# Power tables in channel-pair order, x loaded by segment, and the lag bounce split by PSUM bank, in a kernel of gated attention and a long convolution

## The chip, the cores and the metric

The kernel runs on one core of one Trainium2 chip. Its time is the device time of one execution in microseconds (us). Before the change the median of three runs was 586.04 us (585.66 to 587.24). One further execution was profiled; it took 592.4 us, and the trace of it spans 590.6 us.

## The reference

The result is `g * a + (1 - g) * b` over x with 2048 tokens and 512 channels, where g is a sigmoid of x times gate_w, one number for each token. Cut to what matters:

```
a: 32 heads of 16, four segments of 512 tokens
   in each segment: causal softmax attention, plus a linear-attention read of a
   memory M that holds phi(k)^T v of the segments before; mixed by sigmoid(beta)
   the result times wo
b: K[d, l] = Re sum_n C[d,n] * exp(dt[d] * A[d,n] * l_rounded_to_bf16) * dt[d] * B[d,n]
   y = causal convolution over the 2048 tokens of u[:, d] with K[d, :], by FFT
   b = y + u * Dskip          (u is x)
```

The lag index l goes through bfloat16, so lags beyond 256 are rounded and the kernel needs only five blocks of 128 of them.

## The kernel before, in words

There are three bodies of work.

**Attention.** `do_xT` transposes a segment of x on TensorE. `project`, `seg_tokens`, `seg_state`, `group`, `ophase` and `oproj` do the rest by segment and by eight heads; the exponentials of `group` (L1030) are 160 instructions of 128x1024 on ScalarE. `project` leaves its keys in SBUF through L985 (ScalarE) and L986 (VectorE). `oproj` writes its product, scaled by the token gate, through two SBUF buffers to a DRAM tensor, scr_abuf (L1113 and the DMA behind it). `gate_tokens` computes the token gate for all four segments at once, writes it to DRAM (scr_gbuf), reads it back in another order, and L914 on VectorE takes 1 minus it.

**Tables and lags.** z = exp(dt*A) and its powers z^(2^k), k = 0 to 10, come from `ssm_powers`: per power a tile of three planes (re, im, -im), each 512 columns, one column per channel, with the 128 states n on the partitions. `tables(c)` is called for each of four blocks of 128 channels. It builds a table F of 32 entries and a table G of 49 entries; an entry is a power of z, re and im, for 128 channels. Each of 15 calls of `cmul` makes up to 8 entries out of earlier ones, with three VectorE instructions: product with re (L1145), crossed product with im into a tile t2 (L1148), and the sum (L1151). Then come the lag products: for each channel two matmuls (re and im) with the channel's 32 entries of F as weights and its 49 entries of G as moving data give the 32x49 lags of K for that channel. Those are 256 matmuls for each block, in four PSUM banks of 8 slots by 4 column groups, each bank copied out by L1191. A table holds entry after entry, 128 channels each, so the 32 or 49 values that one matmul reads lie 128 elements (256 bytes) apart in a partition. The lags go to DRAM (scr_K) with one DMA of 392 KB for each block and come back with one DMA in channel order (kd). L1196 and L1199 rearrange kd into a tile kl, five transposes (L1206) and L1209 put it in KTT. Tile kl is taken from the pool of t2.

**x levels and tail.** `x_level1` is the first level of the transform of x, written to DRAM (scr_Z). `tail` loads scr_Z and constants into memory that the tables held before; for t = 0 to 15 it multiplies transform constants with KTT (L1246, L1247), transforms Z (L1263), multiplies both (L1267, L1269, L1271), transforms back, evacuates to a tile V (L1282 or L1284), and stores V to DRAM (scr_V). Every fourth t it loads V2 from there. Last comes the final level with the gate (L1306, L1320).

**What sets the order.** Every instruction is an `op` with an engine, an estimated cost, a key and the tiles it touches. A list scheduler in `Sched.schedule` simulates the engines with those costs and writes each engine's instructions down in the order in which it started them; of those ready at once the lowest key goes first. On the chip each engine works through its own list in order, with semaphore waits. All DMAs are issued by the SP queue, in order too. A tile pool hands its buffers out strictly in the order in which the program asked for tiles: `if self.queue[self.qpos] is not tile or not self.free: return None`. Pools that share memory have phases; a later phase's pool waits until the earlier one's is done. A part of the lines around the change:

```
t2P = mkpool("t2", 4096, 3)
kl = Tile(t2P, BF16)
a = T0            # the prep tiles (pb, ft, xk ...) lie over F, G and t2
KEYS = (12, 6, 50, 70)
```

Of the kernel before, what the change touches and what calls it, by code (L numbers as in the profile page):

```python
# [8 lines left out]
BF16 = mybir.dt.bfloat16  # L9
# [5 lines left out]
NDMA = 110  # L15
KEYS = (12, 6, 50, 70)
# [502 lines left out]
def f_exp(f):  # L519
    if f < 16:  # L520
        return 4 * f
    if f < 24:
        return 2 + 4 * (f - 16)
    return 1 + 2 * (f - 24)
# [51 lines left out]
def build_kernel(nc, A_x, A_wq, A_wk, A_wv, A_wo, A_beta, B_A_re, B_A_im, B_B_re, B_B_im,  # L576
                 B_C_re, B_C_im, B_log_dt, B_Dskip, gate_w, out):
    with contextlib.ExitStack() as es:
# [39 lines left out]
        gzT = S.keep(64, F32)  # L618
        gcolT = S.keep(64, F32)
        g4T = S.keep(64, F32)  # L620
# [7 lines left out]
        smP = S.pool("small", S.addr, 128, 8)  # L628
        S.addr += 8 * 128
# [8 lines left out]
        xTP = mkpool("xT", 4096, 4)  # L638
# [12 lines left out]
        pTP = mkpool("pT", 2048, 8)  # L651
# [3 lines left out]
        oTP = mkpool("oT", 1024, 6)  # L655
# [4 lines left out]
        t2P = mkpool("t2", 4096, 3)  # L660
        T1 = a
        pwP = mkpool("pw", 3072, 11)
# [3 lines left out]
        assert a <= 207 * 1024, a  # L666

        a = T0
# [3 lines left out]
        xkP = mkpool("xk", 4096, 4, 0)  # L672
# [5 lines left out]
        a = T1 + 33792 + 2048  # L678
# [7 lines left out]
        K3P = mkpool("K3", 3072, 2, 2)  # L686
# [3 lines left out]
        VP = mkpool("V", 2048, 2, 2)  # L690
# [37 lines left out]
        xk = []  # L728
        for s in range(4):
            T = Tile(xkP, BF16)  # L730
            S.dma(lambda T=T: ap(T, dims=[[512, 4], [1, 512]]),
                  lambda s=s: bass.AP(x.tensor, x.offset + s * 4 * 128 * 512, [[512, 128], [128 * 512, 4], [1, 512]]),
                  524288, w=[T], key=(-0.95 if s == 0 else 1.0 + s))
            xk.append(T)
# [13 lines left out]
        def do_xT(s):  # L748
            S.tag = "xT"
            T = Tile(xTP, BF16)  # L750
            parts = []
            for hb in range(2):
                P = S.ps(dt=BF16)

                def f(e, P=P, hb=hb):
                    for t2 in range(2):
                        for k in range(4):
                            i = e.transpose(ap(P, t2 * 512 + k * 128, n=128), ap(xk[s], (2 * hb + t2) * 512 + k * 128, n=128), ap(ident, n=128))
                    return i
                op("PE", 8 * 0.07, f, r=[xk[s], ident], w=[P])  # L760
# [51 lines left out]
        def plane(T, i, c0=0, n=512):  # L812
            return ap(T, i * 512 + c0, n=n)

        def ssm_powers(pb, dt, zr, zi):
            S.tag = "pow"
            A = lambda T: ap(T, n=512)
            for k in range(11):
                pw = Tile(pwP, BF16)
                op("ACT", c_act(512), lambda e, pw=pw, zr=zr: e.activation(plane(pw, 0), A(zr), ACT.Copy), r=[zr], pw=[pw])  # L820
                op("ACT", c_act(512), lambda e, pw=pw, zi=zi: e.activation(plane(pw, 1), A(zi), ACT.Copy), r=[zi], pw=[pw])
                op("ACT", c_act(512), lambda e, pw=pw, zi=zi: e.activation(plane(pw, 2), A(zi), ACT.Copy, scale=-1.0), r=[zi], pw=[pw])
# [12 lines left out]
        def ssm_cb(pb, dt):  # L835
# [7 lines left out]
            op("DVE", 0.69, lambda e: e.tensor_tensor(ap(CBT, n=512), A(u1), A(u2), ALU.subtract), r=[u1, u2], pw=[CBT])  # L843
            op("DVE", 0.69, lambda e: e.scalar_tensor_tensor(A(u1), A(pb[4]), -1.0, A(bi), ALU.mult, ALU.mult), r=[bi, pb[4]], w=[u1])
            op("DVE", 0.69, lambda e: e.tensor_tensor(A(u2), A(pb[5]), A(br), ALU.mult), r=[br, pb[5]], w=[u2])
            op("DVE", 0.69, lambda e: e.tensor_tensor(ap(CBT, 512, n=512), A(u1), A(u2), ALU.subtract), r=[u1, u2], pw=[CBT])
            P = S.ps()
            op("PE", c_mm(512), lambda e: mm(e, ap(P, n=512), ap(onesT, n=128), ap(CBT, n=512), True, True), r=[onesT, CBT], w=[P])
# [6 lines left out]
        dK = DT()  # L855
# [39 lines left out]
        def gate_tokens():  # L895
# [3 lines left out]
            def mkf(s):  # L899
                def f(e):  # L900
                    for tb in range(4):
                        for k in range(4):
                            i = mm(e, ap(P, 4 * s + tb, n=1), ap(xT[s], k * 512 + tb * 128, n=128), ap(gwT, k, n=1), k == 0, k == 3)
                    return i
                return f
            for s in range(4):
                op("PE", 0.9, mkf(s), r=[xT[s], gwT], pw=[P])
# [508 lines left out]
```

## Time and profile before

| what | value |
|---|---|
| time, median of 3 runs | 586.04 us |
| profiled execution: time, span | 592.4 us, 590.6 us |
| TensorE busy | 451.5 us (76%), 3837 matmuls |
| VectorE busy | 377.3 us (64%) |
| ScalarE busy | 371.7 us (63%) |
| mean granted TensorE clock | 0.777 |
| DMA | 46.03 MB, 64297 packets |

A row of the timeline gives start and length in us, engine, line, operation and shape; a bracket at its end says how long the engine had been idle before, and who released it. A timeline row with x4 is four instructions from the first one's start to the last one's end. A row of the groups gives busy time in us and the mean in ns, then idle time before them. All matmuls but two kinds run through one helper, L715, so they are told apart by shape: 128x49 on 128*32 weights is the lag product. A row of the windows gives the stretch, its length, then busy time of each engine with the number of instructions that fall into it, and the granted clock.

### The profile page before, as it was taken

How to read it: one execution, taken by the hardware profiler on the slowest of the kernel's cores; microseconds unless marked ns; L12 is line 12 of the kernel's file. 1: busy time of each engine (PE TensorE's matmuls, PEld its weight loads, DVE VectorE, ACT ScalarE, POOL GpSimd, SP SyncE). 2: the span in 40 equal slices, each digit the busy share in tenths (PEclk: the TensorE clock that was granted, in tenths of full speed). 3: DMA queues.
4: the chain of work that ended last, by engine and by line, in shares of the span. 5: the costliest groups of instructions: out<-in, count | busy, mean ns of one | idle time of the engine just before them, and what ended most of it. 6: DMA issues, size and time to landing. Idle time of an engine off the chain costs nothing.

```text
span 590.6 us, 9127 instructions
## 1 busy us (share of the span) xinstructions
PE 451.5 (76%) x3837; PEld 225.3 (38%) x3837; DVE 377.3 (64%) x569; ACT 371.7 (63%) x405; POOL 5.0 (1%) x17
## 2 busy tenths in 40 slices
PE   5846639999888889986998964989945897877080
PEld 3323213336643238534358421358412443323020
DVE  3757738995629998679993379927401395645063
ACT  5989838989864867682899531898744564545000
POOL 1000000000000000000000000000000000000000
PEclk9866677999595765796995585885986899889576
DMA  8600013330190000700000700020999977544616
GB/s 243 166 1 2 2 36 108 116 109 27 16 77 1 0 1 1 29 28 17 21 1 2 34 22 0 2 68 1 101 122 169 359 210 194 158 139 158 158 50 167
DMA packets 64297, 46.03 MB, mean 78 GB/s; under 512 B 28160, under 2 KB 59392, under 8 KB 64000
## 3 DMA queue, kind: packets, MB, share of 16 engines
q1 hardware_dynamic: 64256, 45.44, 36.5%
q8 instruction: 30, 0.49, 0.4%
q14 instruction: 11, 0.09, 0.1%
HBM read 31.23 MB, written 14.20 MB: 77 GB/s over the span
## 4 chain that ended last, share of the span: by engine, by line
PE 28%; DVE 22%; ACT 18%; DMA 18%; SPq 9%; issue 4%; DVEq 0%; ACTq 0%
PE psum L715 27%; SPq L248 9%; ACT sb L1030 6%; DMA scr_V<-sb 5%; ACT sb L1191 5%; DVE sb L1151 5%; DMA scr_K<-sb 4%; DVE sb L1148 4%; DVE sb L1145 4%; DMA sb<-scr_K 2%; DMA scr_gbuf<-sb 2%; DMA sb<-scr_V 2%; DVE sb L1282 1%; DVE sb L879 1%; DMA sb<-in_A_wq_dram 1%
## 5 line engine op out<-in xcount | busy, mean ns | idle before, releaser
L715 PE MATMUL psum<-sb 128*32 128x49 bf16 (+12 forms) x3601 | 432.2, 384 | 115.7 <-ACT sb L1030 24.2
L715 PEld LDWEIGHTS psum<-sb 128*128 128x128 bf16 (+5 forms) x3601 | 207.2, 155 | 335.1 <-issue 123.7
L1030 ACT ACTIVATE sb<-psum 128x1024 bf16<-128x1024 f32 x160 | 189.3, 1236 | 42.5 <-PE psum L715 41.4
L1148 DVE TENSOR_TENSOR sb<-sb 128x2048 bf16<-128x2048 bf16 (+3 forms) x60 | 50.7, 844 | 3.1 <-PE psum L1206 3.1
L1151 DVE TENSOR_TENSOR sb<-sb 128x2048 bf16<-128x2048 bf16 (+3 forms) x60 | 51.0, 850 | 1.8
L1145 DVE TENSOR_TENSOR sb<-sb 128x2048 bf16<-128x2048 bf16 (+3 forms) x60 | 50.4, 845 | 0.1
L1191 ACT ACTIVATE sb<-psum 128x392 bf16<-128x392 f32 x16 | 32.6, 2108 | 3.5 <-PE psum L715 3.5
L1097 DVE CAST sb<-psum 128x512 bf16<-128x512 f32 x16 | 28.6, 1790 | 9.6 <-PE psum L715 9.6
L1113 ACT ACTIVATE sb<-psum,sb 128x512 bf16<-128x512 f32 x16 | 10.9, 687 | 35.6 <-DMA scr_abuf<-sb 20.8
L1246 ACT ACTIVATE sb<-psum 128x1024 bf16<-128x1024 f32 x16 | 16.4, 1023 | 22.5 <-PE psum L715 22.5
L1320 DVE SCALAR_TENSOR_TENSOR sb<-psum,sb 128x512 bf16<-128x512 f32 x16 | 10.9, 744 | 23.5 <-DMA sb<-scr_abuf 18.5
L1081 DVE TENSOR_SCALAR sb<-psum 128x32 f32<-128x32 f32 x12 | 2.2, 187 | 35.8 <-PE psum L715 35.8
L1044 ACT ACTIVATE sb<-psum 128x512 bf16<-128x512 f32 x32 | 19.1, 596 | 5.8 <-PE psum L715 5.7
L1263 ACT ACTIVATE sb<-psum 128x1024 bf16<-128x1024 f32 x16 | 16.2, 1020 | 7.1 <-PE psum L715 3.7
L1282 DVE CAST sb<-psum 128x1024 bf16<-128x1024 f32 x8 | 9.8, 1221 | 15.8 <-DMA scr_V<-sb 12.2
L986 DVE TENSOR_SCALAR sb<-psum,sb 128x512 bf16<-128x512 f32 x16 | 11.8, 745 | 9.0 <-ACT sb L985 8.9
L1062 DVE RECIPROCAL sb<-psum 128x32 f32<-128x32 bf16 x16 | 5.7, 355 | 17.0 <-PE psum L1057 16.9
L982 ACT ACTIVATE sb<-psum 128x512 bf16<-128x512 f32 x16 | 9.5, 596 | 11.0 <-PE psum L715 11.0
L1284 ACT ACTIVATE sb<-psum 128x1024 bf16<-128x1024 f32 x8 | 8.2, 1024 | 11.0 <-PE psum L715 5.6
L985 ACT ACTIVATE sb<-psum,sb 128x512 bf16<-128x512 f32 x16 | 10.9, 684 | 6.5 <-PE psum L715 6.4
L877 ACT ACTIVATE sb<-psum 128x1024 bf16<-128x1024 f32 x8 | 8.2, 1025 | 10.2 <-PE psum L715 10.2
L934 DVE CAST sb<-psum 128x512 bf16<-128x512 f32 x16 | 14.0, 884 | 0.9 <-PE psum L715 0.9
(83 smaller groups left out, 286.1 us busy)
## 6 DMA issues: line engine op xcount, KB each, us to landing
sb<-c_D SPq DMA_DIRECT2D x16, 320.0 KB, 4.4
sb<-in_A_x_dram SPq DMA_DIRECT2D x32, 128.0 KB, 4.1
scr_Z<-sb SPq DMA_DIRECT2D x16, 256.0 KB, 2.2
sb<-scr_Z SPq DMA_DIRECT2D x32, 128.0 KB, 7.3
scr_V<-sb SPq DMA_DIRECT2D x16, 256.0 KB, 3.1
sb<-scr_V SPq DMA_DIRECT2D x16, 256.0 KB
sb<-in_A_x_dram SPq DMA_DIRECT2D x4, 512.0 KB, 7.7
scr_abuf<-sb SPq DMA_DIRECT2D x16, 128.0 KB, 2.5
```

The lines of the kernel that those rows point to most:

```text
L248: return self.op("SP", 0.06, lambda e: e.dma_start(out(), in_(), **kw), r=r, w=w, pw=pw, key=key, lat=lat)
L715: mm = lambda e, o_, l, r_, st, sp, **kw: e.matmul(o_, lhsT=l, rhs=r_, start=st, stop=sp, skip_group_check=True, **kw)
L1030: op("ACT", c_act(1024), lambda e, P=P, pT=pT: e.activation(ap(pT, n=1024), ap(P, n=1024), ACT.Exp, scale=0.25), r=[P], w=[pT])
L1044: op("ACT", c_act(512), lambda e: e.activation(ap(raw, n=512), ap(PV, n=512), ACT.Copy), r=[PV], w=[raw])
L1097: op("DVE", c_dps(512), lambda e: e.tensor_copy(ap(oT, n=512), ap(P3, n=512)), r=[P3], w=[oT])
L1145: op("DVE", c_tt(256 * n), lambda e: e.tensor_tensor(D_(), ap(tile, src * 128, [[pl, 2], [128 * sstep, n], [1, 128]]), ap(pw, d0, [[0, 2], ...
L1148: op("DVE", c_tt(256 * n), lambda e: e.tensor_tensor(T_(), ap(tile, pl + src * 128, [[-pl, 2], [128 * sstep, n], [1, 128]]), ap(pw, sg[0] ...
L1151: op("DVE", c_tt(256 * n), lambda e: e.tensor_tensor(D_(), D_(), T_(), ALU.add), r=[t2], w=wr)
L1191: op("ACT", c_act(392), lambda e, P=P, bk=bk: e.activation(ap(kex, bk * 392, n=392), ap(P, n=392), ACT.Copy), r=[P], pw=[kex])
L1246: op("ACT", c_act(1024), lambda e, PK=PK, K3=K3: e.activation(ap(K3, dims=[[1024, 2], [1, 512]]), ap(PK, dims=[[512, 2], [1, 512]]), ACT.C ...
L1263: op("ACT", c_act(1024), lambda e, PX=PX, Xs=Xs: e.activation(ap(Xs, dims=[[256, 2], [512, 2], [1, 256]]), ap(PX, dims=[[512, 2], [256, 2] ...
L1282: op("DVE", c_dps(1024), lambda e, PI=PI, V=V: e.tensor_copy(ap(V, n=1024), ap(PI, n=1024)), r=[PI], w=[V])
```

## The change

1. **Tables by channel pair.** F and G are stored as [re/im][64 channel pairs][entry][2 channels]. The power tiles become [block][re, re, im, -im][128 channels], 4096 bytes where they had 3072; the two copies of re are one ScalarE instruction and -im comes from VectorE. The lag matmuls then read 32 and 49 values that lie 2 elements (4 bytes) apart. `cmul` keeps its three VectorE instructions and their sizes, with innermost runs of 2 elements in the first two and of 2n in the sum. G holds im first; the sign of the crossed product is the same for F and G. The two interleaved quarters of F become two blocks, and `f_exp` is changed to suit.
2. **x by segment.** x is loaded to one buffer (four before) a segment at a time; `do_xT` and `gate_tokens` are called for each segment inside the attention loop; xT has 2 buffers (4 before). The DMAs of the token gate and L914 come with the last segment.
3. **Lag bounce by bank.** Each block's scr_K store becomes four, one behind each bank's copy; the DRAM dependence is kept by block. Tile kl is taken from the pool of kex, not of t2.
4. **Buffers.** t2 2 (from 3), pT 7 (8), oT 5 (6), small 6 (8); in the tail K3 3 (2) and V 4 (2). The prep tiles lie over G and t2 only, no longer over F.
5. **Planner.** The assumed cost of a lag matmul is 0.04 us (0.033).

```diff
@@ cmul
-                D_ = lambda: ap(tile, dst * 128, [[pl, 2], [128 * dstep, n], [1, 128]])
-                T_ = lambda: ap(t2, dims=[[n * 128, 2], [128, n], [1, 128]])
-                sg = (1, 512) if conj else (2, -512)
-                op("DVE", c_tt(256 * n), lambda e: e.tensor_tensor(
-                    D_(), ap(tile, src * 128, [[pl, 2], [128 * sstep, n], [1, 128]]),
-                    ap(pw, d0, [[0, 2], [0, n], [1, 128]]), ALU.mult), r=rd + [pw], w=wr + [tile])
...
+                run = lambda T, E, e0, st: ap(T, 2 * e0, [[2 * E, 128], [2 * st, n], [1, 2]])
+                pwv = lambda i: ap(pw, c * 512 + i * 256, [[2, 128], [0, n], [1, 2]])
+                op("DVE", c_tt(256 * n), lambda e: e.tensor_tensor(run(tile, ne, dst, 1), run(tile, ne, src, sstep), pwv(0), ALU.mult),
+                   r=rd + [pw], w=wr + [tile])
+                op("DVE", c_tt(256 * n), lambda e: e.tensor_tensor(run(t2, n, 0, 1), run(tile, ne, src, sstep), pwv(1), ALU.mult),
+                   r=rd + [pw], w=[t2])
+                D_ = lambda: ap(tile, 2 * dst, [[ne * 128, 2], [2 * ne, 64], [1, 2 * n]])
                 op("DVE", c_tt(256 * n), lambda e: e.tensor_tensor(
-                    D_(), D_(), T_(), ALU.add), r=[t2], w=wr)
+                    D_(), D_(), ap(t2, n * 128, [[-n * 128, 2], [2 * n, 64], [1, 2 * n]]), ALU.add), r=[t2], w=wr)
@@ the lag products and the bounce
-                                    i = mm(e, ap(P, sl * 49, n=49, p0=32 * dq, np_=32), ap(F, cc * FPL + dl, [[128, 32]]),
-                                           ap(G, cc * GPL + dl, [[128, 49]]), cc == 0, cc == 1, tile_position=(0, 32 * dq))
+                                    i = mm(e, ap(P, sl * 49, n=49, p0=32 * dq, np_=32), ap(F, cc * FPL + (dl // 2) * 2 * NF + dl % 2, [[2, NF]]),
+                                           ap(G, (1 - cc) * GPL + (dl // 2) * 2 * NG + dl % 2, [[2, NG]]), cc == 0, cc == 1, tile_position=(0, 32 * dq))
-            S.dma(lambda: bass.AP(Kdr, c * 32 * 128 * 49, [[49, 128], [128 * 49, 32], [1, 49]]), lambda: ap(kex, dims=[[49, 32], [1, 49]]),
-                  401408, r=[kex], w=[dK], packets=4096)
+                S.dma(lambda bk=bk: bass.AP(Kdr, (c * 32 + bk * 8) * 128 * 49, [[49, 128], [128 * 49, 8], [1, 49]]),
+                      lambda bk=bk: ap(kex, bk * 392, [[49, 8], [1, 49]]), 100352, r=[kx], pw=[dK[c]], packets=1024)
-            kl = Tile(t2P, BF16)
+            kl = Tile(kexP, BF16)
@@ ssm_powers
-                op("ACT", c_act(512), lambda e, pw=pw, zi=zi: e.activation(plane(pw, 2), A(zi), ACT.Copy, scale=-1.0), r=[zi], pw=[pw])
+                op("DVE", c_ts4(512), lambda e, pw=pw: e.tensor_scalar(
+                    ap(pw, 384, [[512, 4], [1, 128]]), ap(pw, 256, [[512, 4], [1, 128]]), -1.0, None, ALU.mult), r=[pw], pw=[pw])
@@ the loop over segments
-        for s in range(1, 4):
-            S.key = 8.0 + s
-            do_xT(s)
-        S.key = 20.0
-        gate_tokens()
...
+                if hg == 0:
+                    if s > 0:
+                        S.key = TA0 + GA * (i0 - 3)
+                        do_xT(s)
+                    S.key = TA0 + GA * (i0 + 1)
+                    gate_tokens(s)
@@ pools
-        xTP = mkpool("xT", 4096, 4)
+        xTP = mkpool("xT", 4096, 2)
+        xkP = mkpool("xk", 4096, 1)
-        t2P = mkpool("t2", 4096, 3)
+        t2P = mkpool("t2", 4096, 2)
-        VP = mkpool("V", 2048, 2, 2)
+        VP = mkpool("V", 2048, 4, 2)
```

152 lines of the change are left out of this document (76 added, 76 removed).

## The prediction

> **What bounds the kernel now.** I read the page's busy times and chain first, then the windows by stage, then TensorE's waits, then the timeline around them.
>
> ```profile
> PE 451.5 (76%) x3837; PEld 225.3 (38%) x3837; DVE 377.3 (64%) x569; ACT 371.7 (63%) x405; POOL 5.0 (1%) x17
> PE 28%; DVE 22%; ACT 18%; DMA 18%; SPq 9%; issue 4%; DVEq 0%; ACTq 0%
> ```
>
> ```profile
> 100.00:300.00 200.00, 177.96 (x1608) 91.82 (x1608) 163.73 (x235) 147.99 (x154) 2.16 (x6) 0.80 0.21 35
> 300.00:460.00 160.00, 126.51 (x1186) 70.37 (x1183) 85.73 (x132) 105.46 (x93) 0.49 (x2) 0.71 0.43 53
> 460.00:560.00 100.00, 69.70 (x536) 31.14 (x533) 52.34 (x82) 43.89 (x46) 0.00 (x0) 0.89 0.65 194
> ```
>
> No engine is full over the whole span, but TensorE (the first busy figure) is busy 178.0 of 200 us between 100 and 300 us, 126.5 of 160 after that, and 69.7 of 100 in the tail. The chain mixes all engines. So the time is TensorE's work plus the holes that other engines and DMAs leave in it; I price the change by both. Its waits name the holes:
>
> ```profile
> PE psum L715 <- DVE sb L986: 16.1, 5, 13.1
> PE psum L715 <- DMA sb<-scr_V: 15.2, 1, 15.2
> PE psum L715 <- ACT sb L1113: 13.3, 2, 12.5
> PE psum L715 <- DVE sb L879: 9.6, 2, 9.3
> ...
> PE psum L715 <- DVE sb L1282: 4.8, 1, 4.8
> ```
>
> Each is few waits with one long one, so each has one cause, found below.
>
> **The lag products.** One half of one block's burst:
>
> ```profile
> L715 PE MATMUL psum<-sb 128*32 128x49 bf16 x1024 | 67.9, 499 | 2.8 <-DVE sb L986 1.5 <-ACT sb L982 1.2
> ```
>
> ```profile
> 34.81 1.81 PE L715 MATMUL psum<-sb 128*128 128x1 bf16 x40 [0.79 <-DVE sb L764]
> ...
> 305.94 8.39 DVE L992 TENSOR_SCALAR sb<-sb 128x512 bf16<-128x512 bf16 x1
> ...
> 315.51 8.95 PE L715 MATMUL psum<-sb 128*32 128x49 bf16 x128 [1.23 <-ACT sb L982]
> ...
> 327.69 0.29 DVE L992 TENSOR_SCALAR sb<-sb 128x512 bf16<-128x512 bf16 x1
> ```
>
> ```profile
> 150.40:158.60 8.20, 8.20 (x128) 8.18 (x128) 8.20 (x1) 8.20 (x2) 0.00 (x0) 0.50 0.01 2
> 306.00:314.00 8.00, 8.00 (x128) 7.93 (x128) 8.00 (x2) 8.00 (x2) 0.00 (x0) 0.73 0.02 4
> ```
>
> A weight load and its lag matmul take 67.9/1024 = 66 ns of TensorE. At a granted clock of 0.50 128 pairs take 8.2 us, at 0.73 8.0 us, so the array's clock isn't what sets the 66 ns; and while a burst runs, a VectorE instruction that takes 0.29 us elsewhere takes 8.39 us. Both point to reads at 256-byte steps that hold up whoever else reads SBUF. The nearest pair whose operands aren't so spread is the token gate's: 40 pairs in 1.81 us, 45 ns, with four times the weight columns. I take 45 ns: 67.9 - 1024 x 0.045 = 21.8 us less on TensorE. The bounds are 66 ns (nothing gained) and, as an estimate for a quarter of the columns, half of 45 ns (45 us less). The stalls of ScalarE and VectorE go too, but they lie beside TensorE's burst, so I count nothing for them.
>
> [...]
>
> **The table products on VectorE.** 180 instructions keep their sizes; L1145 and L1148 get innermost runs of 2 elements, L1151 longer ones.
>
> ```profile
> L1145 DVE TENSOR_TENSOR sb<-sb 128x2048 bf16<-128x2048 bf16 x28 | 34.1, 1218 | 0.0
> L1148 DVE TENSOR_TENSOR sb<-sb 128x2048 bf16<-128x2048 bf16 x28 | 34.1, 1217 | 0.0
> ...
> L1145 DVE TENSOR_TENSOR sb<-sb 128x1024 bf16<-128x1024 bf16 x16 | 10.9, 684 | 0.0
> ...
> L1282 DVE CAST sb<-psum 128x1024 bf16<-128x1024 f32 x8 | 9.8, 1221 | 15.8 <-DMA scr_V<-sb 12.2 <-PE psum L715 3.6
> ...
> L1306 DVE TENSOR_TENSOR sb<-sb 128x2048 bf16<-128x2048 bf16 x4 | 9.2, 2288 | 3.2 <-PE psum L715 3.2
> ```
>
> ```profile
> 14.42 0.43 DVE L801 TENSOR_SCALAR sb<-sb 128x512 f32<-128x512 f32 x1
> ...
> 23.03 0.42 DVE L891 COPY sb<-sb 128x512 f32<-128x512 f32 x1
> ```
>
> Bounds: as now (1.22 us), or one element for each cycle as L1306 has it (2.29 us). The second would add 56 x 1.07 = 60 us, and 32 x 0.54 = 17 us for the 1024s (1.22 against 0.68): 77 us, small ones left out. A run of 2 still fills a 4-byte word, and the new power operand repeats one word n times; L891 reads one word 16 times over (the gate, spread to 16 columns) and takes the 0.42 us of a contiguous read of that size. So I take 1.22 us and no cost, covered anyway by VectorE's idle time (163.7 busy of 200 us, stalls included). If that cover is gone, each 0.1 us on the 88 large ones costs 9 us.
>
> [...]
>
> **The bounce and tile kl.** Two holes of TensorE hang on them.
>
> ```profile
> 341.24 0.62 DVE L1199 COPY sb<-sb 128x128 bf16<-128x128 bf16 x5
> 341.77 0.42 DVE L1148 TENSOR_TENSOR sb<-sb 128x512 bf16<-128x512 bf16 x1
> ...
> 361.90 0.74 DVE L986 TENSOR_SCALAR sb<-psum,sb 128x512 bf16<-128x512 f32 x1
> ...
> 362.70 3.84 PE L715 MATMUL psum<-sb 128*128 128x512 bf16 x14 [13.13 <-DVE sb L986]
> ```
>
> ```profile
> 417.09 0.45 SPq L248 DMA_DIRECT2D scr_K<-sb  x1
> 417.58 12.28 SPq L248 DMA_DIRECT2D sb<-scr_Z  x1
> ```
>
> ```profile
> 447.53 0.69 ACT L1113 ACTIVATE sb<-psum,sb 128x512 bf16<-128x512 f32 x1 [12.78 <-DMA scr_abuf<-sb]
> 448.12 1.02 ACT L1030 ACTIVATE sb<-psum 128x1024 bf16<-128x1024 f32 x1
> 448.25 6.57 SPq L248 DMA_DIRECT2D scr_abuf<-sb  x2
> 448.28 5.59 PE L715 MATMUL psum<-sb 128*128 128x136 bf16 x34 [12.53 <-ACT sb L1113]
> ```
>
> kl stands in t2's pool, which serves in program order, so a block's first L1148 can't start before the block before has its lags back: 341.77 follows L1199 at 341.24. VectorE then works off 20 us of late products, and L986 waits behind them in its list, and TensorE 13.1 us for L986. With kl in kex's pool the products run while the lags bounce. I count -13.1 us (bounds 0 and that).
>
> At the end the DMA behind the last scr_K store sat 12.28 us in SP's queue; behind it sat the abuf stores, so that L1113 found no buffer and TensorE waited 12.5 us. A quarter of the packets behind the last bank should hold SP a quarter as long, 3.1 us: -9.2 us (bounds 0 and -12.5). The 12 added issues, 0.45 us each as at 417.09, are passed by x loads, abuf stores and scr_Z stores; SP has room for 5.4 us spread over 300.
>
> **The tail.** V gets four buffers, so L1282 needn't wait for the store of two steps before:
>
> ```profile
> 521.18 1.23 DVE L1282 CAST sb<-psum 128x1024 bf16<-128x1024 f32 x1 [5.83 <-DMA scr_V<-sb]
> ...
> 524.72 9.13 PE L715 MATMUL psum<-sb 128*128 128x512 bf16 x60 [4.42 <-DVE sb L1271]
> ```
>
> TensorE's 4.4 us here and its 4.8 us on L1282 above come from such waits: -9.2 us. The 15.2 us for the last V2 load stay: that load follows the last store in any order.
>
> **Moved work.** 48 transposes of x go from the start, where TensorE waits on ScalarE anyway, into the full stage:
>
> ```profile
> 32.72 1.31 PE L758 MATMUL psum<-sb 128*128 128x128 bf16 x16
> ```
>
> 82 ns each, 3.9 us more there. The gate's DMAs and L914 go to the last segment:
>
> ```profile
> 84.23 0.17 DVE L914 TENSOR_SCALAR sb<-sb 128x16 f32<-128x16 f32 x1 [9.87 <-DMA sb<-scr_gbuf]
> ...
> 86.73 13.34 PE L715 MATMUL psum<-sb 128*128 128x512 bf16 x80 [9.31 <-DVE sb L879]
> ```
>
> VectorE stands 9.87 us at L914, an evacuation is queued behind it, and TensorE loses 9.3 us. Moved past every other step of VectorE's list, the same stand-still should recur in the last segment, with L986 and L1097 behind it: 0 net (bounds: -9.3 if it falls into idle time, +9.3 if it holds up more). The 11 negations moved to VectorE and the smaller gate steps lie under the stage bounded by ScalarE's powers; nothing counted. Fewer buffers of pT, oT and xT could add waits; the shown waits name none of them, so I count nothing, with the 13.1 us of the largest planner hole as the upper bound.
>
> **Sum.** -21.8 - 13.1 - 9.2 - 9.2 + 3.9 = -49.4 us. From the profiled 592.4 us that gives 543.0; the median of the runs is 6.4 us below the profiled time, so 536.6, rounded 537. Check by shares: in 300 to 460 us the holes are 33.5 us; less 13.1 and 9.2 that leaves 11.2 beside 126.5 - 10.9 us of work, 91% busy, about what 100 to 300 us shows already (89%).
>
> **The rivals.** (1) The stride doesn't set the 66 ns; the pair's issue does, and the lag term is nothing: 537 + 22 = 559. For it: the time is the same at two clocks, as an issue limit would also make it. Against: 45 ns for the gate's pairs, and the neighbours' stalls. (2) The tables, no longer tied to the bounce, run ahead, and TensorE is busy 95% from 100 to 460 us: (178.0 + 126.5 - 21.8)/0.95 = 298 us for 360, 62 us less, and 9.2 in the tail, 3.9 back: 592.4 - 67 - 6.4 = 519. For it: every stage's work is there to fill holes with. Against: planner and chip differ, as the 13.1 us hole shows. (3) Slower: runs of 2 elements take VectorE to one element a cycle. It is priced above at 77 us, in tables that stand in VectorE's list between the attention's evacuations: 537 + 77 = 614 with all of it exposed, 575 with half. It decides from 64% exposed, 49.4 of 77 us. For it: the first two instructions lose their long rows. Against: full words, and L891. [...]
>
> **How the numbers follow.** Forecast 0.55; rival 1 0.17; rival 2 0.15; rival 3 0.10, mostly slower; 0.03 for no change by a mixture. The time is the likeliest case's, 537. The range goes from 508 (rival 2 with half of the further lag gain of 23 us) to 572 (rival 1 and a hole of 13.1 us): rival 3 and the very best cases stay out. Runs of this kernel differ by about 0.3%. Faster 0.88, within 0.3% 0.03, slower 0.09.
>
> **What would show it.** Right: 128x49 matmuls at about 46 us in all instead of 67.9, L992 and L1097 near their short times during bursts, L1145 and L1148 at 1.22 us, first L1148 of a block ahead of L1199 of the one before, no 12 us issue in SP's queue, no L1282 wait on scr_V, L914's wait late. Wrong: L1145 above 1.5 us; 128x49 still near 66 ns; a new hole of 10 us or more behind L914, xT or scr_K issues.

## The result, and the profile after

The changed kernel takes 513.64 us, the median of four runs (510.9 to 517.56), against 586.64 us (585.66 to 588.02) for the kernel before in the same job: a ratio of 0.8759, 95% interval 0.8696 to 0.8823. The profiled execution took 510.9 us, its span 509.1 us, so 81.5 us of the span are gone. Four more runs, in a later job, gave 502.1 to 511.19 us. Over both jobs the runs of this one kernel spread by 3%, where the prediction took 0.3%, and that limits what the experiments below can say by totals.

Where did the 81.5 us go? First the busy times on the page of the changed kernel, then its windows over the two middle stages.

```profile
PE 376.7 (74%) x3801; PEld 165.1 (32%) x3837; DVE 341.1 (67%) x586; ACT 310.8 (61%) x397; POOL 4.5 (1%) x17
```

```profile
100.00:300.00 200.00, 161.99 (x2014) 74.13 (x2029) 166.94 (x290) 131.45 (x170) 2.37 (x8) 0.89 0.23 41
300.00:460.00 160.00, 125.17 (x1227) 55.15 (x1238) 85.58 (x150) 90.75 (x106) 0.00 (x0) 0.84 0.68 146
```

TensorE is busy 376.7 us where it was 451.5: 74.8 us of the 81.5. (The profile lacks 36 of the 3837 matmul records; a second profile of the same kernel has all of them and 377.8 us.) Its holes are almost as large as they were, 509.1 - 376.7 = 132.4 us against 590.6 - 451.5 = 139.1. So on balance TensorE's work got shorter and its waits hardly did. The groups say which work (busy us, mean ns of one, idle time ahead); the last row is the kernel before.

```profile
L720 PE MATMUL psum<-sb 128*32 128x49 bf16 x1024 | 12.1, 201 | 7.5 <-DVE sb L988 3.4 <-issue 3.0 <-DVE sb L881 0.7
L1153 DVE TENSOR_TENSOR sb<-sb 128x256 bf16<-128x256 bf16 x8 | 3.1, 386 | 0.2
L1099 DVE CAST sb<-psum 128x512 bf16<-128x512 f32 x16 | 11.0, 687 | 7.4 <-PE psum L720 7.4
```

```profile
L1097 DVE CAST sb<-psum 128x512 bf16<-128x512 f32 x16 | 28.6, 1790 | 9.6 <-PE psum L715 9.6
```

The lag products went from 67.9 to 12.1 us, 55.8 us and 12 ns for a pair of weight load and matmul. (The other 19 us lie in matmuls that were not edited, 364.6 us where they took 383.6. The granted clock, 0.837 where it was 0.777, doesn't account for them: in the first experiment below, with as many records missing, they take 358.8 us at 0.797. Their cause stays open.) The large table products keep their 1.22 us; the small ones, of 256 columns, don't, as the first experiment shows. L1099, L1097 before, takes 687 ns where it took 1790: the neighbours of a burst no longer stall.

TensorE's longest waits show what the holes are now.

```profile
PE psum L720 <- DVE sb L1067: 10.9, 3, 10.0
PE psum L1210 <- DVE sb L1203: 10.1, 1, 10.1
PE psum L720 <- DMA sb<-scr_V: 10.1, 1, 10.1
PE psum L720 <- DVE sb L988: 9.4, 5, 4.1
```

L988 is the old L986, and its longest wait fell from 13.1 to 4.1 us. The longest wait for L1113 (now L1115) fell from 12.5 to 6.0 us, that for the last V2 load from 15.2 to 10.1, and the 4.8 us on L1282 are gone. Two of 10 us are new. The timeline shows the first one's origin, the gate:

```profile
318.46 0.36 SPq L249 DMA_DIRECT2D scr_gbuf<-sb  x1
330.09 2.67 SPq L249 DMA_DIRECT2D sb<-scr_gbuf  x4
335.04 0.18 DVE L916 TENSOR_SCALAR sb<-sb 128x16 f32<-128x16 f32 x1 [11.01 <-DMA sb<-scr_gbuf]
336.49 4.21 PE L720 MATMUL psum<-sb 128*128 128x512 bf16 x138 [10.02 <-DVE sb L1067]
```

SP stands from 318.8 to 330.1 us until the gate's store has landed, VectorE stands 11 us at L916, and L1067 behind it holds TensorE. The second is the last block's bounce:

```profile
341.51 7.41 SPq L249 DMA_DIRECT2D scr_K<-sb  x3
348.95 0.58 SPq L249 DMA_DIRECT2D sb<-c_M  x1
349.57 11.81 SPq L249 DMA_DIRECT2D sb<-scr_Z  x8
361.43 2.35 SPq L249 DMA_DIRECT2D scr_K<-sb  x1
363.82 12.60 SPq L249 DMA_DIRECT2D sb<-scr_Z  x15
...
377.19 7.68 SPq L249 DMA_DIRECT2D sb<-scr_Z  x9
385.03 1.18 SPq L249 DMA_DIRECT2D sb<-scr_K  x1
```

```profile
395.74 0.72 PE L1210 MATMUL psum<-sb 128*128 128x128 bf16 x5 [10.12 <-DVE sb L1203]
```

The lag products of the last block end at 344 us, but nine tail loads stand in SP's list ahead of its fourth store, and 24 more ahead of the load that brings the lags back. The transposes of the lags start at 395.74 us.

### The profile page after: what moved, and what is told of

Its sections match the earlier page's. It is cut to its first block, busy times and chain, and to the rows that moved or that the text cites. A ratio compares the mean times of both kernels' runs of the same rounds, so it can differ in the third digit from the quotient of the medians.

```text
span 509.1 us, 9111 instructions
## 1 busy us (share of the span) xinstructions
PE 376.7 (74%) x3801; PEld 165.1 (32%) x3837; DVE 341.1 (67%) x586; ACT 310.8 (61%) x397; POOL 4.5 (1%) x17
## 4 chain that ended last, share of the span: by engine, by line
PE 31%; DVE 28%; DMA 17%; ACT 12%; SPq 6%; issue 4%; DVEq 0%; ACTq 0%
PE psum L720 29%; SPq L249 6%; DVE sb L1153 5%; DVE sb L1150 5%; DVE sb L1148 4%; ACT sb L1032 3%; DMA scr_K<-sb 3%; DMA sb<-in_A_x_dram 2%; DMA scr_gbuf<-sb 2%; DMA scr_abuf<-sb 2%; DMA sb<-c_D 2%; ACT sb L819 2%; DMA sb<-scr_V 2%; DMA sb<-scr_K 1%; DVE sb L881 1%
## 5 line engine op out<-in xcount | busy, mean ns | idle before, releaser
L720 PE MATMUL psum<-sb 128*32 128x49 bf16 (+15 forms) x3565 | 357.1, 292 | 92.1 <-ACT sb L1032 17.1
L720 PEld LDWEIGHTS psum<-sb 128*128 128x128 bf16 (+5 forms) x3601 | 146.1, 101 | 298.3 <-issue 125.5
L1032 ACT ACTIVATE sb<-psum 128x1024 bf16<-128x1024 f32 x160 | 158.0, 1028 | 40.0 <-PE psum L720 38.5
L1153 DVE TENSOR_TENSOR sb<-sb 128x2048 bf16<-128x2048 bf16 (+3 forms) x60 | 51.8, 864 | 1.8
L1148 DVE TENSOR_TENSOR sb<-sb 128x2048 bf16<-128x2048 bf16 (+3 forms) x60 | 51.2, 857 | 0.1
L1150 DVE TENSOR_TENSOR sb<-sb 128x2048 bf16<-128x2048 bf16 (+3 forms) x60 | 51.3, 855 | 0.0
L1250 ACT ACTIVATE sb<-psum 128x1024 bf16<-128x1024 f32 x16 | 16.4, 1023 | 24.2 <-PE psum L720 24.2
L1115 ACT ACTIVATE sb<-psum,sb 128x512 bf16<-128x512 f32 x16 | 11.0, 687 | 24.5 <-PE psum L720 17.4
L1310 DVE TENSOR_TENSOR sb<-sb 128x2048 bf16<-128x2048 bf16 x4 | 9.1, 2289 | 19.4 <-PE psum L720 18.8
L1046 ACT ACTIVATE sb<-psum 128x512 bf16<-128x512 f32 x32 | 19.1, 597 | 2.8 <-PE psum L720 2.8
L1267 ACT ACTIVATE sb<-psum 128x1024 bf16<-128x1024 f32 x16 | 16.2, 1021 | 4.6 <-PE psum L720 4.6
L1059 PE MATMUL psum<-sb 128*128 128x128 bf16 x128 | 12.9, 260 | 7.2 <-ACT sb L1115 6.0
L1286 DVE CAST sb<-psum 128x1024 bf16<-128x1024 f32 x8 | 9.8, 1224 | 11.9 <-PE psum L720 11.9
L988 DVE TENSOR_SCALAR sb<-psum,sb 128x512 bf16<-128x512 f32 x16 | 11.9, 745 | 6.5 <-ACT sb L987 6.5
L1099 DVE CAST sb<-psum 128x512 bf16<-128x512 f32 x16 | 11.0, 687 | 7.4 <-PE psum L720 7.4
L1195 ACT ACTIVATE sb<-psum 128x392 bf16<-128x392 f32 x16 | 7.4, 501 | 13.5 <-PE psum L720 11.1
L881 DVE CAST sb<-psum 128x1024 bf16<-128x1024 f32 x8 | 9.8, 1223 | 7.0 <-PE psum L720 6.8
L1059 PEld LDWEIGHTS psum<-sb 128*128 128x128 bf16 x128 | 10.5, 120 | 9.5 <-ACT sb L1115 6.2
```

The source lines that it names most:

```text
L720: mm = lambda e, o_, l, r_, st, sp, **kw: e.matmul(o_, lhsT=l, rhs=r_, start=st, stop=sp, skip_group_check=True, **kw)
L881: op("DVE", c_dps(1024), lambda e, P=P, zs=zs: e.tensor_copy(ap(zs, n=1024), ap(P, n=1024)), r=[P], w=[zs])
L988: op("DVE", c_dps(512), lambda e, P=P: e.tensor_scalar(ap(ko, n=512), ap(P, n=512), ap(mkT, 1, n=1), None, ALU.mult), r=[P, mkT], w=[ko])
L1032: op("ACT", c_act(1024), lambda e, P=P, pT=pT: e.activation(ap(pT, n=1024), ap(P, n=1024), ACT.Exp, scale=0.25), r=[P], w=[pT])
L1046: op("ACT", c_act(512), lambda e: e.activation(ap(raw, n=512), ap(PV, n=512), ACT.Copy), r=[PV], w=[raw])
L1059: i = e.transpose(ap(P, tb * 256 + gi * 128, n=128), ap(ra[gi], tb * 128, n=128), ap(ident, n=128))
```

## The experiments

**Theories.** Mine after the result: the operands' distance in SBUF sets the lag products' time, and the lag term was right in kind and too small; the rest of the change is worth some 25 us in holes. Rivals: the 74.8 us come from the other edits, or the near reads only matter because their neighbours stall less.

**The layout alone, undone and done.** First the changed kernel with F and G entry after entry again, nothing else altered:

```diff
-   ap(F, cc * FPL + (dl // 2) * 2 * NF + dl % 2, [[2, NF]])
+   ap(F, cc * FPL + dl, [[128, NF]])       # G likewise; cmul's views to suit
```

> The changed kernel with tables F and G stored entry after entry again, same instructions in the same planned order, so that only the addresses differ. If the distance between the values that a lag matmul reads is what counts: 128x49 matmuls back from 12 us to about 67 us in all, short VectorE and ScalarE instructions stretched to some 8 us during bursts, time 514 + 55 = 569 us or a little more (560 to 585). If the gain came from the new order and buffers and the bursts merely ran at a better moment: 128x49 stays under 30 us and the time under 530 us.

558.08 us (553.19 to 565.12, before 588.62 in that job), just under the 560 to 585 expected. Its groups:

```profile
L720 PE MATMUL psum<-sb 128*32 128x49 bf16 x1024 | 69.0, 503 | 5.5 <-DVE sb L988 3.7 <-ACT sb L984 1.0 <-DVE sb L881 0.7
L1148 DVE TENSOR_TENSOR sb<-sb 128x2048 bf16<-128x2048 bf16 x28 | 34.1, 1216 | 0.0
L1153 DVE TENSOR_TENSOR sb<-sb 128x256 bf16<-128x256 bf16 x8 | 2.3, 291 | 0.2
L1099 DVE CAST sb<-psum 128x512 bf16<-128x512 f32 x16 | 17.8, 1110 | 5.5 <-PE psum L720 5.5
```

The lag products are back at 69.0 us, 57 us more, and the time rises by 44 us (by its two shortest runs, 553.2 and 553.6, by 40). L1148 of 2048 columns takes the same time with rows of 128 as with runs of 2 elements, 1216 and 1215 ns. The instructions of 256 columns don't: L1153 takes 291 ns with rows of 128, 386 with the pairs. They make a single entry, so each run of 2 elements, one 4-byte word, is followed by a hop of 196 bytes to the next pair of channels. Over 24 such instructions (L1148, L1150, L1153) that costs VectorE 2.2 us in all, 0.66 to 0.74 ns a word. Then the kernel before with near reads in its lag matmuls and no other edit:

```diff
-   ap(F, cc * FPL + dl, [[128, 32]])
+   ap(F, cc * FPL + (dl // 2) * 64 + dl % 2, [[2, 32]])     # G likewise
```

> The kernel before with one edit: the lag matmuls read 32 and 49 values 4 bytes apart instead of 256, out of the unchanged entry-major tables, so they multiply other table values (this part of the computation is changed). Tables, VectorE patterns, bounce and buffers are as before. Distance theory: 128x49 falls from 68 us to about 12 us and the time by 56 us or somewhat less where other engines set the pace: 530 to 555 us. If the gain needs the bounce, kl and V edits: not below 570 us.

531.23 us (528.08 to 534.66), ratio 0.9062 (0.8967 to 0.9156), as the distance theory expected. Its busy times and its group of lag products:

```profile
PE 376.8 (71%) x3800; PEld 167.7 (32%) x3837; DVE 336.7 (63%) x569; ACT 312.3 (59%) x405; POOL 5.0 (1%) x17
...
L715 PE MATMUL psum<-sb 128*32 128x49 bf16 x1024 | 11.7, 198 | 4.3 <-issue 2.7 <-DVE sb L986 1.1 <-ACT sb L982 0.4
```

And two of TensorE's waits in it (us in all, times, longest):

```profile
PE psum L715 <- DVE sb L986: 16.9, 5, 14.4
PE psum L715 <- ACT sb L1113: 16.8, 2, 16.0
```

Near reads alone bring 57 us, and 67.9 - 11.7 = 56 us are off TensorE's lag products. That the two are alike is no proof of one for one: TensorE's busy time falls by 451.5 - 376.8 = 74.7 us, as much as in the whole change, and its holes grow from 139.1 to 532.2 - 376.8 = 155.4 us. Nor are the neighbours out of it: ScalarE is busy 312.3 us where it was 371.7. So near reads are shown to be the cause of the 57 us; what of it is TensorE's own time and what the neighbours' freed time isn't separated. The holes that the edits of kl and of the bounce aim at are still there. The rest of the change is then worth 531 - 514 = 17 us on top of near reads (the intervals of the two ratios don't overlap), or 588.6 - 558.1 = 30.5 us without them.

**How near is near.** In two kernels each of the four blocks reads at another step: in the first, block 0 has weights at 256 bytes and moving data at 4, block 1 the reverse, blocks 2 and 3 both at 16 and at 32; in the second, both at 2, 8, 64 and 128 bytes; other entries of the tables are multiplied than the lags need.

```diff
-   ap(F, cc * FPL + (dl // 2) * 2 * NF + dl % 2, [[2, NF]])
+   ap(F, cc * FPL + dl, [[(128, 2, 8, 16)[c], NF]])    # G: (2, 128, 8, 16)
+   ap(F, cc * FPL + dl, [[(1, 4, 32, 64)[c], NF]])     # G: the same; second kernel
```

> The changed kernel with another read step in the lag matmuls of each block (other table values are multiplied: this part of the computation is changed). Block 0: weights 256 bytes apart, moving data 4. Block 1: weights 4, moving data 256. Block 2: both 16 bytes. Block 3: both 32 bytes. Theory that both operands' reads are slow when far: blocks 0 and 1 each lie between 12 and 66 ns a pair, shares by 32 and 49 values. Rival, only the moving data counts: block 0 as fast as now (12 ns), block 1 at about 66. [...]

> As the run before, both operands with the same step. Block 0: 2 bytes (contiguous), block 1: 8 bytes, block 2: 64 bytes, block 3: 128 bytes. [...] Theory of collisions at large power-of-two steps: a gradual rise from 64 to 128 to 256 bytes. If 4 bytes already costs something against contiguous reads, block 0 is under 12 ns.

The rows are weight loads on TensorE, length and count; a quotient is the time of a load with its matmul. In blocks 2 and 3 of the first kernel the rows of loads take in some of other matmuls, so two copies of one bank after another (L1195 on ScalarE) stand in for them: from one to the next lie 64 pairs. First kernel (523.86 us, one run), blocks 0 to 3:

```profile
128.51 1.49 PEld L720 LDWEIGHTS psum<-sb 128*32 128x32 bf16 x48 [0.42 <-issue]
191.64 2.55 PEld L720 LDWEIGHTS psum<-sb 128*32 128x32 bf16 x64 [2.64 <-DVE sb L988]
...
273.50 0.50 ACT L1195 ACTIVATE sb<-psum 128x392 bf16<-128x392 f32 x1 [1.06 <-PE psum L720]
275.07 0.50 ACT L1195 ACTIVATE sb<-psum 128x392 bf16<-128x392 f32 x1 [1.07 <-PE psum L720]
...
352.71 0.50 ACT L1195 ACTIVATE sb<-psum 128x392 bf16<-128x392 f32 x1 [2.07 <-PE psum L720]
354.25 0.50 ACT L1195 ACTIVATE sb<-psum 128x392 bf16<-128x392 f32 x1 [1.05 <-PE psum L720]
```

Second kernel (512.19 us, one run), blocks 0 to 3, and an unbroken burst of the changed kernel:

```profile
128.20 0.44 PEld L720 LDWEIGHTS psum<-sb 128*32 128x32 bf16 x48 [0.42 <-issue]
188.24 0.83 PEld L720 LDWEIGHTS psum<-sb 128*32 128x32 bf16 x64 [2.44 <-DVE sb L988]
258.57 6.82 PEld L720 LDWEIGHTS psum<-sb 128*32 128x32 bf16 x256 [0.21 <-issue]
334.67 9.80 PEld L720 LDWEIGHTS psum<-sb 128*32 128x32 bf16 x256 [0.41 <-issue]
```

```profile
339.38 1.20 PEld L720 LDWEIGHTS psum<-sb 128*32 128x32 bf16 x128 [0.41 <-issue]
```

| step of both operands, bytes | 2 | 4 | 8 | 16 | 32 | 64 | 128 | 256 |
|---|---|---|---|---|---|---|---|---|
| ns a pair | 9 | 9 | 13 | 24 | 24 | 27 | 38 | 63 |

(The 4-byte value is from the last row, the 256-byte value from the prediction's window of 128 pairs in 8.00 us. The 12 and 66 ns above are the groups' busy time by count, ends of bursts included.) With one operand far and the other near a pair takes 31 ns (weights far) or 40 ns (moving data far); 31 + 40 less the 9 of two near ones is 62, close to the 63. So it isn't near or far: the time about doubles between 8 and 16 bytes (13 to 24 ns), stands nearly flat to 64 (27 ns), and more than doubles again to 256 (63 ns). The theory of collisions expected the rise from 64 to 256 bytes (27, 38 and 63 ns) and says nothing of the one from 8 to 16. All the steps that were run are powers of two, so it isn't shown that collisions make this rise, nor what makes the first one.

The second kernel also bears on the question that was left open. Its lag products take 24.2 us, 12 us more than in the changed kernel, its neighbours hardly stall (ScalarE is busy 311.5 us, there 310.8), and yet its one run lies among the changed kernel's 502 to 518. That speaks against a gain of one for one by TensorE's own time; one run isn't enough to show it.

**The bounce in one store.** The changed kernel with one 392 KB store for each block, where the fourth stood:

```diff
-   bass.AP(Kdr, (c * 32 + bk * 8) * 128 * 49, [[49, 128], [128 * 49, 8], [1, 49]])
-   ap(kex, bk * 392, [[49, 8], [1, 49]])
+   bass.AP(Kdr, c * 32 * 128 * 49, [[49, 128], [128 * 49, 32], [1, 49]])
+   ap(kex, dims=[[49, 32], [1, 49]])
```

> The changed kernel with one part undone: a block's lags go out in one store of 392 KB where the fourth of the four stores stood, and the other three are dropped; every engine's order is otherwise the same. The prediction's term (a store by bank holds SP a quarter as long, -9.2 us) expects SP to stand about 12 us behind the last block's store again, against the 2.35 us and 12.60 us for 15 loads now, and the time to rise by about 9 us, to 523 us. Rival: the four stores end no earlier than one did, since the loads of Zx stand between them in SP's order, and the store isn't late because of its size; then 514 us, within 3 us, and the 10 us wait of the L1210 transposes stays as it is.

517.91 us (513.95 to 523.06), ratio 0.874 (0.8598 to 0.8882). The changed kernel has 0.8759 and, in the later job, 0.8646 (0.8559 to 0.8732): no difference can be told by totals. The trace (of the longest of the four runs) has one, but in another block than the prediction's:

```profile
218.69 0.71 PE L1214 MATMUL psum<-sb 128*128 128x128 bf16 x5 [6.47 <-DVE sb L937]
```

These are the second block's transposes (L1210 in the changed kernel). They come 16.7 us behind the end of that block's lag products, in the two profiles of the changed kernel 11.0 and 11.1, and TensorE waits 6.5 us for them. In the last block, where the prediction put its gain, the same stretch is 48.5 us with one store, 51.6 and 48.5 with four, and 42.7 in the kernel before: nothing was won there. SP's list above shows why: the load of the last block's lags stands behind 24 other loads in any case. So the split shortens one bounce by some 6 us; whether that reaches the total isn't shown.

**kl tied to the tables again.**

```diff
+   klp.append(kl)                                       # at the end of tables(c)
-   r=rd + [pw], w=[t2])                                 # L1150
+   r=rd + [pw] + (klp if nstep[0] > 3 and S else []), w=[t2])
-   op("PE", 0.5, ft_, r=[kl, ident], w=[P])             # L1210
+   op("PE", 0.5, ft_, r=[ident], w=[P, kl])
```

> The changed kernel with the old tie put back: the third product of each block of tables (its L1150 instruction) waits until the transposes of the block before have read kl, as when kl stood in t2's pool with its three buffers; the planner places the work anew with that wait. The prediction's term (-13.1 us for the untying) expects a TensorE hole of about 13 us on L988 and a time near 527 us. Rival: in the changed kernel VectorE has the products early but then stands 18.4 us in all at the L1200 copies, waiting for the same load of the lags, so the untying moved the stand-still and gained little: 514 to 518 us.

524.56 us (517.54 to 528.09), ratio 0.8835 (0.864 to 0.9031). By medians 11 us above the changed kernel, near the 13.1 us of the prediction, but the intervals of the ratios overlap, and the plan was made anew. No hole on L988 came back (its longest wait is 4.1 us, as in the changed kernel). The trace shows the loss elsewhere. VectorE's waits for the loaded lags, in all 18.4 us in the changed kernel and 9.1 the longest, are here:

```profile
DVE sb L1204 <- DMA sb<-scr_K: 29.4, 3, 18.9
```

From the end of the first block's lag products to the start of the second's it takes 68.2 us, in the two profiles of the changed kernel 53.2 and 52.3, and in the kernel before, which has the tie, 60.6. So the next block's tables do come later with the tie, as the prediction argued; TensorE's wait for L988 isn't the place where that shows.

**Two buffers of V.** Each evacuation also waits for the store of two steps before.

```diff
+   S.vcp[t].alld = S.vcp[t].alld + [S.vst[t - 2]]      # t = 2 to 15
```

> The changed kernel with one part undone: the evacuation of PI into V at step t waits for the store of V at step t-2, as with two buffers of V; every order is the same. The prediction's term (-9.2 us) expects VectorE to wait some 12 us in all at L1286 for scr_V stores and the time near 523 us. Rival: the tail is set by its loads and by TensorE's start at 397 us, the wait for the last V2 load (10.1 us now, 15.2 before) takes up what the buffers give, and the time stays at 514 us, within 2 us.

524.95 us (520.66 to 526.59), ratio 0.8867 (0.8703 to 0.9032). Here the trace says more than the total, since all orders are the same and the tail is a stretch of its own. VectorE's wait for the stores, and the timeline with start and end of the stretch:

```profile
DVE sb L1286 <- DMA scr_V<-sb: 17.0, 3, 6.0
```

```profile
395.79 0.71 PE L1210 MATMUL psum<-sb 128*128 128x128 bf16 x5 [8.88 <-DVE sb L1203]
...
477.90 5.80 PE L720 MATMUL psum<-sb 128*128 128x512 bf16 x20 [7.10 <-DVE sb L1275]
492.62 2.28 PE L720 MATMUL psum<-sb 128*128 128x512 bf16 x6 [8.91 <-DMA sb<-scr_V]
```

From the L1210 transposes to the end of the wait for the last V2 load it takes 492.62 - 395.79 = 96.8 us; in the changed kernel 83.2 (478.91 - 395.74), in its second profile 82.2. Four buffers of V are worth 13.7 us, or 14.6 by the second profile. Three holes of 5.2, 4.7 and 7.1 us lie in between, where the changed kernel has 0.9, 1.4 and 3.1.

**The two new holes.** If the gate's hole and the bounce's hole are in series with all else, moving the waiting steps should win 20 us. First L916 alone, to the head of the tail in VectorE's list:

```diff
+   l = [o for o in S.prog["DVE"] if o is not S.g4]         # S.g4: L916
+   i = min(j for j, o in enumerate(l) if o.tag == "K0")    # the tail's first step
+   S.prog["DVE"] = l[:i] + [S.g4] + l[i:]
```

> The changed kernel with the gate's L916 instruction alone moved, from before the last segment's evacuations to the head of the tail in VectorE's list; its DMAs stay where they are. If the 11.0 us that VectorE stands at L916 for its load, and the 10.0 us that TensorE then waits for L1067, set the time, it falls by 8 to 10 us, to 505 us. Rival: the last block's lags then go out 10 us earlier but the loads of Zx in SP's order still hold the last store and the load of kd, so that the hole ahead of the L1210 transposes grows by as much, from 10.1 to some 20 us, and the time stays at 512 to 514 us.

508.94 us (505.63 to 510.9), ratio 0.8605 (0.8488 to 0.8722): not to be told from the changed kernel, whose profiled span of 509.1 us it shares. Its trace:

```profile
340.32 0.86 PE L720 MATMUL psum<-sb 128*32 128x49 bf16 x64 [7.32 <-ACT sb L1115]
```

VectorE no longer stands, but SP does, at the same store, with the abuf stores behind it; L1115 then finds no buffer, and TensorE waits 7.3 us for that. The transposes come at 396.71 us, in the changed kernel at 395.74. So the next kernels move entries of SP's list, beside the changed kernel itself for a mark: in the first the fourth store comes right behind the third and the load of the lags behind the first nine tail loads; in the second the gate's four loads go behind that, and L916 to the tail.

```diff
+   early = [S.kst[3, 3]] + tl[:9] + [S.kld[3]]     # fourth store, c_M and 8 scr_Z, load of the lags
+   S.prog["SP"] = sp[:last + 1] + early + [o for o in sp[last + 1:] if o not in early]
+   S.prog["SP"] = sp[:i] + g + sp[i:]              # second kernel: the gate's four loads, i behind S.kld[3]
```

> The changed kernel unaltered, as the mark beside which the two others of this job are read; runs of it so far went from 510.9 to 517.56 us. Expected: the same, ratio to the kernel before 0.87 to 0.88.

> The changed kernel with SP's list alone altered, in the last block: the fourth scr_K store comes right behind the third, and the load of the lags right behind M2 and the first eight loads of Zx, ahead of the other 24. If the 10.1 us that TensorE stands ahead of the L1210 transposes comes from the place of that store and load in SP's order, the load is issued near 363 us instead of 385, the hole goes, and the time falls by about 10 us, to 504 us (with the 1.2 us behind the transposes 11). Rival: the loads of Zx that come later now hold up the tail's first products, or the wait for the last V2 load grows from 10.1 us by as much, and the time stays at 512 to 514 us.

> As the kernel with the last block's SP order altered, and besides the gate's four scr_gbuf loads go behind the load of the lags in SP's list and L916 goes to the head of the tail in VectorE's list, so that neither queue stands for the gate's 11 us. With L916 alone moved, SP still stood those 11 us with the abuf stores behind it, L1115 found no buffer, TensorE waited 7.3 us there and the L1210 transposes came at the same time as before. If the two holes are in series, the gate's 10 us and the bounce's 10 us are both won: 494 us, within 4 us. Rival: with the gate's wait gone TensorE is bound by ScalarE's powers between 330 and 385 us, and only the bounce's 10 us are won, 504 us.

The three took 507.5 us (502.1 to 511.19; ratio 0.8646, 0.8559 to 0.8732), 510.36 us (509.5 to 511.61; 0.8675, 0.8618 to 0.8732) and 514.0 us (513.87 to 521.18; 0.8765, 0.8681 to 0.8849). Neither gain came; of the first, the rival did. The first of the two:

```profile
369.57 14.98 PE L720 MATMUL psum<-sb 64*64 64x256 bf16 x112 [6.32 <-DMA sb<-scr_Z]
388.23 0.71 PE L1210 MATMUL psum<-sb 128*128 128x128 bf16 x5 [0.48 <-DVE sb L1203]
```

The hole ahead of L1210 is gone (0.48 us), and a wait for scr_Z, 6.32 us, has taken its place: the loads that were moved back are now the late ones. L1210 comes at 388.2 us, in the mark at 388.0. The second:

```profile
379.76 0.45 PE L1210 MATMUL psum<-sb 128*128 128x128 bf16 x5 [0.92 <-DVE sb L1203]
398.68 4.49 DVE L1310 TENSOR_TENSOR sb<-sb 128x2048 bf16<-128x2048 bf16 x2 [18.37 <-DMA sb<-in_A_x_dram]
405.56 11.40 PE L720 MATMUL psum<-sb 128*128 128x512 bf16 x85 [16.75 <-DVE sb L1275]
```

Now L1210 is 8 us earlier, at 379.76, and the next wait in line takes it all back: the first two L1310 stand ahead of the tail's products in VectorE's list and wait 18.4 us for x. The last kernel moves those x loads and L1310s into the tail as well:

```diff
+   S.prog["SP"] = sp[:i] + S.xl[:8] + sp[i:j] + S.xl[8:] + sp[j:]   # behind scr_V stores 5 and 11
+   S.prog["DVE"] = l[:i] + u + l[i:]                                # u: S.uo[:2]; behind V's ninth evacuation
```

> As the kernel with the last block's SP order and the gate altered, and besides the 16 second loads of x go from ahead of the tail's products in SP's list to behind the fifth and the eleventh scr_V store, eight each, and the first two L1310 products, which stand ahead of the tail in VectorE's list and waited 18.4 us for those loads, go behind the ninth evacuation of V. In that kernel the lags were transposed at 379.8 us of the span, against 388.0 us in the unaltered one beside it, but TensorE then stood 16.8 us for L1275, behind L1310. If that stand-still took the gain, it goes: 514.0 - 16.8 = 497 us, within 4 us, ratio to the kernel before about 0.845, and no TensorE wait of more than 5 us between 380 and 450 us. Rival: the 2 MB of x now meet the V stores and V2 loads in the tail, the wait for the last V2 load grows from 9.5 us or V's evacuations wait, and the time stays above 505 us.

511.9 us (506.49 to 515.83), ratio 0.87 (0.8621 to 0.878): a miss by 15 us; the time stays above 505 us, as the rival said.

```profile
424.83 8.28 PE L720 MATMUL psum<-sb 128*128 128x512 bf16 x56 [6.01 <-DMA sb<-c_D]
437.70 9.54 PE L720 MATMUL psum<-sb 128*128 128x512 bf16 x60 [4.59 <-DVE sb L1275]
```

The 16.75 us wait is gone. In its place TensorE waits 6.0 us for c_D, behind the x loads in SP's list, and 4.6 us for L1275, behind the moved L1310s in VectorE's. Two stretches, from the timelines, put the kernels side by side:

| kernel | L1210 starts at, us | from there to the end of the V2 wait, us | sum |
|---|---|---|---|
| changed, two profiles | 395.7; 388.0 | 83.2; 82.2 | 478.9; 470.3 |
| SP order | 388.2 | 89.3 | 477.6 |
| SP order and gate | 379.8 | 101.9 | 481.7 |
| x later too | 380.9 | 97.9 | 478.8 |

What is won ahead of L1210 comes back behind it. The windows of 345 to 385 us, of the changed kernel and of the one with x later, show what these waits have in common (the last two figures are the DMA engines' mean busy share, the time that packets took, and GB/s):

```profile
345.00:385.00 40.00, 35.68 (x290) 14.27 (x289) 8.76 (x23) 25.35 (x29) 0.00 (x0) 0.68 1.17 178
```

```profile
345.00:385.00 40.00, 28.36 (x270) 12.70 (x268) 8.97 (x27) 22.58 (x26) 0.00 (x0) 0.80 1.12 148
```

The share is 1.1 to 1.2 in that stretch, whatever the order. It passes 1 (1.17 and 1.12 in these two rows), so packets overlap and it is no plain occupancy; and bytes alone don't make it, for in the mark 330 to 345 us moved 241 GB/s at 0.83, and 345 to 385 us 177 GB/s at 1.19. The tail's loads can't start before the last lag products have freed their memory, and then c_M, 32 loads of scr_Z, the lags and x compete; whichever stands last is waited for. That the transfers and not SP's order bound this stretch is the reading that fits all four kernels; it wasn't tested, neither with fewer bytes nor with fewer packets.

## Why the prediction was right, and which terms were not

537 us was forecast, with a range of 508 to 572; the sign is right, the size 23 us short. The lag term was 34 us too small, and what the rest brought on top, 17 us, was 10.6 us less than its terms of 27.6; so two misses partly cancel. The result lies 6 us inside the range's lower end, and that end came from a rival whose mechanism isn't there, with half of a further lag gain. That the range held is in part luck. By the prediction's steps:

- **The lag products** (-21.8 us): right mechanism, mis-sized term. The step that failed is the choice of the token gate's pair, 45 ns, as the nearest row, with half of it as the lower bound. Measured are 12 ns a pair and -55.8 us, outside the bounds of 0 and -45. The nearest row by shape was no measure of the price by step. Whether the neighbours' stalls were rightly counted at nothing stays open: ScalarE and VectorE are freed by 59 and 41 us with near reads alone, and their part in the 57 us wasn't separated.
- **The table products on VectorE** (no cost): right within 2.2 us; the large ones take 1215 and 1216 ns against 1218 and 1217. In the two calls that read every second entry one word is followed by a hop of 8 bytes, and no table product of 2048 columns took over 1.23 us. The prediction overlooked the two calls of a single entry, with hops of 196 bytes, where the price of 0.66 to 0.74 ns a word is paid.
- **kl** (-13.1 us): the tie put back costs 11 us by medians, within the scatter of zero, and delays the second block's lag products by 15 us. The hole on L988 went, as forecast, but stays away with the tie too, so it isn't shown that kl's pool removed it. VectorE still stands 18.4 us in all at L1200, in four waits of which one is 9.1 us.
- **The bounce by bank** (-9.2 us): not shown. The 12.5 us wait for L1113 went (6.0 us is the longest left), but one store in place of four moves the time by nothing that can be told; it lengthens the second block's bounce by 5.6 us and not the last one's. The prediction overlooked that the load of the lags stands behind the tail's loads in SP's list; the hole of 10.1 us there is new.
- **V** (-9.2 us): right and a little small, 13.7 us by the stretch of the tail. The wait for the last V2 load stayed, as forecast, 10.1 us where it was 15.2.
- **The gate** (0 net): right, 9.3 us went at the start and 10.0 us came at L916 in the last segment. That a hole of 10 us behind the gate or the scr_K issues would prove the forecast wrong was put too strongly: both came, and the lag term outweighed them.
- **Sum.** The lag term was 34 us too small; the terms for holes, -27.6 us with the moved transposes, answer to 30.5 us without near reads and to 17 us with them. That with shorter bursts other work, late beside them before, became the bound would explain the smaller figure; it wasn't tested.
- **Rivals.** The first, that the stride doesn't set the 66 ns, falls by both layout kernels. The second forecast 519 us, nearest to the result, for a reason that isn't there: TensorE is busy 81% and 78% of the two middle stages, not 95%. The third, a slower VectorE, falls but for the 2.2 us: L1148 and L1150 of 2048 columns keep 1.22 us and don't come near the 2.29 us of L1306. The neighbours' stalls, which stood against the first, go with the layout too: L1099 takes 1110 ns with far reads and 687 with near ones, in kernels of one order.

## What to carry to other kernels

Lay the operands of small matmuls out so that neighbouring values of one read lie at most 8 bytes apart: here a pair of 32 weight columns and 49 moving ones took 9 to 13 ns up to that step, 24 at 16 and 32 bytes, 27 at 64, 38 at 128 and 63 at 256. Where transfers compete in one stretch, moving one waiting step in a queue moved the wait to the next, three times here; look first for transfers to save, or for memory that could be free earlier, which was not tried here. Where runs of a kernel spread by 3%, measure small terms on a stretch of the trace whose ends are the same in both kernels, and on two profiles of one kernel for its own scatter (83.2 and 82.2 us for the tail here).

## What was not expected of the hardware

A weight load of 32 columns with a matmul of 49 takes 9 ns at a step of 2 or 4 bytes, with four column groups in turn, and the time goes up in two stages, 13 to 24 ns between 8 and 16 bytes and 27 to 63 ns between 64 and 256. In the rows that follow, the neighbours are slow beside far reads alone, whether one operand is far or both. Two rows of VectorE in the first of the step kernels, the first beside moving data at 256 bytes, the second beside operands at 16 bytes:

```profile
191.50 2.23 DVE L936 CAST sb<-psum 128x512 bf16<-128x512 f32 x1
...
270.25 0.29 DVE L993 TENSOR_SCALAR sb<-sb 128x512 bf16<-128x512 bf16 x1
```

L936 takes 0.69 us elsewhere in that kernel, and L993 0.28; beside block 0, with the weights alone at 256 bytes, L993 takes 1.17 and 1.70 us. The bank copies L1195, 0.50 us beside steps of 16 and 32 bytes, average 2.11 us in the kernel before (L1191). At 128 bytes it is little: one L1032 takes 1.60 us, where 1.02 is usual. So at 16 bytes a pair takes TensorE 24 ns where it takes 13 at 8 bytes, and L993 and L1195 beside it, 0.29 and 0.50 us, are no slower.
